# A transformer block in fp32 on one core: constant matmuls at the start, modulation vectors summed on GpSimd, maxima in sixes, five score banks at the end

## The chip, the core and the metric

The kernel runs on one core of a Trainium2 chip. Its engines are TensorE (PE in the profile, its weight loads PEld), VectorE (DVE), ScalarE (ACT), GpSimd (POOL) and SyncE (SP, which here only issues DMAs). The metric is the device time in microseconds, the median of several runs; lower is better.

## The reference

One token batch x of 2048 rows and 512 columns goes through an attention and a gated MLP. Both are modulated by six vectors that come from a condition c:

```
mod = (silu(c) @ w_mod).reshape(1, 6, 1, 512)      # sa, ca, ga, sb, cb, gb
h = layernorm(x) * (1 + ca) + sa
q, k, v = split(h @ wqkv)                          # 32 heads of 16
x = x + ga * (softmax(q k^T / 4) v) @ wo
h = layernorm(x) * (1 + cb) + sb
x = x + gb * ((silu(h @ w_gate) * (h @ w_up)) @ w_down)   # inner width 1792
```

Everything is fp32. The softmax subtracts the maximum of each row of scores.

## The kernel before

**Precision.** A matmul of two fp32 operands is done as three matmuls of rounded parts (high x high, high x low, low x high), collected in one bank of PSUM by `mm3`. With four slices of 128 of the inner dimension this makes 12 matmuls of 128x512 for one bank: a job. The eight banks are tiles `banks[0..7]` (63 to 70 in the lists of instructions below). `Turn` objects hand them out in a fixed circle: `four` for turned tiles and maxima, `bank` for projections and scores, `single` for bank 7.

**Front.** The rows of x come in four chunks of 512. For chunk 0 the row statistics and the normalized rows are made while the first columns of w_mod are loaded in two halves (`wm_ab`). `mod_part` multiplies silu(c) with such a half on TensorE (four 32-row strips side by side, one for each slice of the inner dimension) and copies the result to SBUF as `ev`; `mod_col` turns it into columns and adds the four strips. `turn` transposes the normalized rows; `modulate` scales and shifts them into `h32`, and `half_prep` splits them into the high and low halves `hT`. Jobs of K and Q start as soon as the first half of `hT` is there.

**Projections.** For chunks 0 to 2, `Stream.jobs` writes out the jobs one matmul at a time, and after each matmul `tick` lets other generators ("lanes", each with a period in matmuls) write one step: the splitting of weights (`w`), the preparation of the next chunk (`p`), and the later modulation vectors (`m`, `mods`): vectors 4 and 3 beside chunk 1, vectors 2 and 5 beside chunk 2. What a lane has not done when the jobs are out is written by `finish` behind them. A post of each job copies the bank by ScalarE, subtracts by VectorE (L369) and stores the parts to DRAM (`qd`, `kd`, L372 and L373), all on SP's queue. V stays in SBUF (L395).

**The first maxima.** Scores are computed twice: once (`max_one`, L479) for the maximum of each row (L481, VectorE), and once, transposed, with the maximum as an extra row of the inner dimension, for the exponential (`score`, L526, and ScalarE's L528). The maxima run 21 steps (`LEAD`) ahead of the scores. So 80 maxima stand alone before the first score; they are written between the jobs `late` that remain of the projections (216 matmuls). They need `qop` and `kop`, loaded from `qd` and `kd` on SP's queue (L404). `side` holds small steps that turn a unit's maxima into a row: `max_rows` by TensorE, `max_turned` by VectorE and eight small DMAs.

**Attention and MLP.** `plain` writes steps of score, max and probabilities times V (L541); `filled` writes scores with matmuls of the output projection and MLP of the previous chunk between them (L739). For the last 80 scores there is no max beside them. There `ALONE` gives other places for the MLP's matmuls, and `bank` gets a longer circle. TensorE executes its instructions in the order in which they are written, as does each engine; a `manual_schedule` keeps that order, and semaphores make an instruction wait for what it reads or for the bank that it overwrites.

## Time and profile before

| | us |
|---|---|
| median of three runs (1864.34 to 1866.59) | 1865.5 |
| the profiled execution | 1862.89 |
| its span, first to last instruction | 1861.0 |
| TensorE busy | 1832.9 |
| VectorE busy | 1542.6 |
| ScalarE busy | 1245.7 |
| GpSimd busy | 414.9 |
| first modulation matmul (L279) starts | 10.78 |
| third projection job starts (L209) | 26.65 |
| first max (L479) starts | 127.78 |
| first score (L526) starts | 188.03 |

A busy time is the union of an engine's instructions in the span. A row of the timeline gives the start, the length, the engine, the line, the operation with what it writes and reads, how often in a row it comes, and in brackets how long the engine idled before and what ended that. The chain of waits goes back from the last instruction to what released it; its rows give start, length and what. A row of windows gives, for a stretch of time, the busy time and the number of instructions of PE, PEld, DVE, ACT and POOL, the granted clock of TensorE, the busy share of the DMA engines and the GB/s that they moved. A row of the groups gives the line, engine, operation and shapes, the count, the busy time in us and the mean of one in ns. TensorE's ends are modelled, so its busy time holds short waits too.

### The profile page before, as it was taken

The page shows a single profiled execution, that of the slowest core. Times are in us where ns is not written, and L with a number is a line of the kernel's source. Part 1 is how long each engine was busy: PE and PEld are TensorE (multiplying, and loading weights), DVE is VectorE, ACT ScalarE, POOL GpSimd, SP SyncE. Part 2 cuts the span into 40 slices and gives each one's busy share as a digit, 9 for nine tenths or more (in the row PEclk, how much of TensorE's full clock was granted, in tenths as well). Part 3 has the DMA queues.
Part 4 walks back from the last instruction along what each step waited for, and adds up shares of the span by engine and source line. Part 5 has one row for each costly group of instructions (what it writes and reads, how often), then busy time and mean ns, then how long its engine had stood idle before and what let it go on. Part 6 is the DMA issues. An engine that isn't in the chain of part 4 may idle for free.

```text
span 1861.0 us, 41049 instructions
## 1 busy us (share of the span) xinstructions
PE 1832.9 (98%) x16906; PEld 1152.3 (62%) x16906; DVE 1542.6 (83%) x2588; ACT 1245.7 (67%) x2391; POOL 414.9 (22%) x498
## 2 busy tenths in 40 slices
PE   7999999999999999999999999999999999999999
PEld 5766444444455667666555667666554576666887
DVE  5558999999999889889999998989999998821543
ACT  4231888888887777767877777777878877773211
POOL 3000454446422211111133111111123011130200
PEclk9999999999999999999999999999999999999999
DMA  8855677766853534654454454454633536243642
GB/s 290 292 200 143 175 179 179 202 168 182 218 98 78 142 99 111 166 118 96 105 130 114 106 132 134 123 123 81 165 79 56 113 89 168 76 166 114 260 177 106
DMA packets 80475, 267.62 MB, mean 144 GB/s; under 512 B 19464, under 2 KB 24104, under 8 KB 59608
## 3 DMA queue, kind: packets, MB, share of 16 engines
q1 hardware_dynamic: 61440, 180.10, 33.3%
q0 software_dynamic: 18160, 84.10, 19.1%
q8 instruction: 133, 2.18, 0.5%
q10 hardware_dynamic: 688, 0.80, 0.1%
q14 instruction: 54, 0.44, 0.1%
HBM read 201.85 MB, written 62.13 MB: 142 GB/s over the span
## 4 chain that ended last, share of the span: by engine, by line
PE 93%; DVE 2%; ACT 2%; DMA 2%; SPq 0%; issue 0%; ACTq 0%; DVEq 0%
PE bank L541 27%; PE bank L526 23%; PE bank L739 19%; PE bank L479 10%; PE bank L749 6%; PE bank L209 6%; DVE mx L481 1%; DVE stt L765 1%; PE bank L162 0%; PE bank L723 0%; DMA wm_ab<-in_w_mod 0%; PE bank L491 0%; PE bank L279 0%; DMA kop<-o_dr 0%; DMA rb<-d_dr 0%
## 5 line engine op out<-in xcount | busy, mean ns | idle before, releaser
L481 DVE TENSOR_REDUCE mx<-bank 128x1 f32<-128x512 f32 x2048 | 1283.8, 681 | 104.1 <-PE bank L479 64.8
L479 PE MATMUL bank<-kop,qop 48*128 48x512 f32 x2048 | 745.0, 431 | 3.2 <-DVE mx L481 1.9
L526 PE MATMUL bank<-qop,kop 50*128 50x512 f32 x2048 | 738.1, 427 | 4.6 <-ACT pt__20559 L528 0.5
L526 PEld LDWEIGHTS bank<-qop,kop 50*128 50x128 f32 x2048 | 345.6, 184 | 305.5 <-issue 63.1
L479 PEld LDWEIGHTS bank<-kop,qop 48*128 48x128 f32 x2048 | 343.0, 184 | 29.2 <-DVE mx L481 14.5
L739 PE MATMUL bank<-act,wgu 64*128 64x512 f32 x1872 | 296.8, 392 | 0.0
L739 PEld LDWEIGHTS bank<-act,wgu 64*128 64x128 f32 x1872 | 187.0, 187 | 30.6 <-issue 0.2
L568 POOL TENSOR_TENSOR on<-o,rb 128x512 f32<-128x512 f32 x31 | 39.7, 1282 | 438.2 <-DMA rb<-d_dr 372.5
L739 PE MATMUL bank<-wd,mid 64*128 64x512 f32 x912 | 136.9, 397 | 0.0
L801 POOL CAST mid<-m 128x512 fp32r<-128x512 f32 x40 | 24.3, 609 | 421.9 <-DVE m L799 161.5
L739 PEld LDWEIGHTS bank<-wd,mid 64*128 64x128 f32 x912 | 93.9, 185 | 11.7 <-issue 0.7
L209 PE MATMUL bank<-hT,wqs 128*128 128x512 f32 x384 | 95.6, 399 | 2.3 <-ACT hT L328 1.0
L209 PEld LDWEIGHTS bank<-hT,wqs 128*128 128x128 f32 x384 | 70.3, 188 | 24.3 <-issue 6.1
L797 DVE SCALAR_TENSOR_TENSOR q<-th,bank 128x512 f32<-128x512 f32 x56 | 37.7, 673 | 55.0 <-ACT th L793 55.0
L793 ACT ACTIVATE th<-bank 128x512 f32<-128x512 f32 x56 | 33.2, 594 | 58.4 <-PE bank L749 58.4
L813 DVE TENSOR_TENSOR x<-bank,x 128x512 f32<-128x512 f32 x84 | 53.8, 684 | 20.3 <-PE bank L526 20.2
L369 DVE TENSOR_TENSOR prt<-bank,prt 128x512 fp32r<-128x512 f32 x32 | 22.0, 688 | 46.8 <-ACT prt L367 44.5
L367 ACT CAST prt<-bank 128x512 fp32r<-128x512 f32 x32 | 18.8, 587 | 59.9 <-PE bank L209 46.8
L799 DVE TENSOR_TENSOR m<-bank,q 128x512 f32<-128x512 f32 x56 | 38.7, 691 | 21.1 <-PE bank L749 19.1
L749 PE MATMUL bank<-wd,mid 128*128 128x512 f32 x216 | 52.3, 394 | 0.5 <-DVE mid L802 0.3
L802 POOL TENSOR_TENSOR mid<-m,mid 128x512 fp32r<-128x512 f32 x40 | 51.6, 1289 | 3.3
L739 PE MATMUL bank<-wgu,act 64*128 64x512 f32 x288 | 47.7, 394 | 0.1
(6286 smaller groups left out, 5129.2 us busy)
## 6 DMA issues: line engine op xcount, KB each, us to landing
wgu<-gu_dr SPq DMA_DIRECT2D x48, 1024.0 KB
wd<-wd_dr SPq DMA_DIRECT2D x28, 1024.0 KB
kop<-kd SPq DMA_DIRECT2D x33, 768.0 KB
kop<-kd POOLq DMA_DIRECT2D x29, 768.0 KB, 8.6
gu_dr<-wgu POOLq DMA_DIRECT2D x14, 1024.0 KB, 14.2
kd<-prt SPq DMA_DIRECT2D x16, 512.0 KB
qd<-prt SPq DMA_DIRECT2D x16, 512.0 KB
kop<-gu_dr SPq DMA_DIRECT2D x8, 1024.0 KB
```

The source lines that it names most:

```text
L209: nc.tensor.matmul(pt, lhs(a, k), rhs(b, k), start=(n == 0), stop=(n == 3 * nk - 1))
L479: nc.tensor.matmul(pm, qop[u][rows, s, qt * P:(qt + 1) * P], kop[u % 3][rows, s, kc * CW:(kc + 1) * CW], start=True, stop=True)
L481: nc.vector.tensor_reduce(mx[u][:, b, s, qt, kc:kc + 1], pm, op=ALU.max, axis=AX.X)
L526: nc.tensor.matmul(sp, kop[u % 3][rows, h // 2, kt * P:(kt + 1) * P], qop[u][rows, h // 2, :], start=True, stop=True)
L541: nc.tensor.matmul(pv[u][32 * h:32 * h + 32, cols], v_flat[:, e0:e0 + 32], p_[h][:, cols], start=(kt == 0 and half == 0), stop=(kt == 15), ...
L568: mul.tensor_mul(on, o, rb)
L739: nc.tensor.matmul(outs[e], lhs(e, a, k)[rows], rhs(b, k)[rows], start=(ph == 0 and j == 0), stop=(j == z and (ph == 1 or trade is not None)),
L749: nc.tensor.matmul(outs[e], lhs(e, a, k), rhs(b, k), start=(j == 0), stop=(j == z))
L797: nc.vector.scalar_tensor_tensor(q, th, 1.0, outs[0], op0=ALU.add, op1=ALU.mult)
L799: nc.vector.tensor_mul(m32, outs[1], q)
L802: (nc.gpsimd if slow else nc.vector).tensor_sub(mid[:, 1, :], m32, mid[:, 0, :].bitcast(F32))
L813: nc.vector.tensor_add(ch.x2[:, t, :], outs[e], ch.x2[:, t, :])
```

## The change

Four edits, at the two ends of the program.

1. Front. TensorE gets 14 matmuls of a constant tile (128x256) at the very start, into banks 0 to 3. All four turned tiles of chunk 0 are written ahead of the second `mod_part`. The circle `bank` has four banks for chunk 0. In the first K and Q jobs `mm3` takes two slices of the inner dimension together, with the low half of `hT` last.
2. Vectors 4, 3, 2 and 5 of the modulation are summed on GpSimd (`mod_sum`: four multiplications by silu(c), two additions in place), and TensorE only adds over the 128 partitions: `sum_col` with four matmuls of one column, `sum_row` with one matmul that spreads the sum to all rows. All four run in one lane with a period of 7.
3. The first 80 maxima. Of the late projections 22 instead of 48 matmuls stand ahead of them; then six maxima on six banks and 14 matmuls by turns, the last 12 matmuls behind the maxima. A unit's maxima are taken so that its first 32 use only the first half of the keys. Unit 0's row of maxima is turned by `max_turned`, two side steps at a time.
4. For the last scores the circle of banks is 4, 5, 0, 1, 2 instead of 4, 5, 0, 1, 5, 0, 4, 1.

```diff
+    busy = pa.tile([P, CW], F32, name="busy", tag="h32", bufs=2)
+    nc.vector.memset(busy[:, 0:2 * P], 1.0)
+    for i in range(14):
+        nc.tensor.matmul(banks[i % 4][:, 0:2 * P], busy[:, 0:P], busy[:, 0:2 * P], start=True, stop=True)
...
-    def mm3(pt, lhs, rhs, nk):
+    def mm3(pt, lhs, rhs, nk, by=1):
         n = 0
-        for k in range(nk):
-            for a, b in ((0, 0), (0, 1), (1, 0)):
+        terms = ((0, 0), (0, 1), (1, 0)) if by == 1 else ((0, 0), (1, 0), (0, 1))
+        for k0 in range(0, nk, by):
+            for (a, b), k in product(terms, range(k0, k0 + by)):
...
+    def mod_sum(wm):
+        for k in range(NK):
+            nc.gpsimd.tensor_scalar_mul(wm[:, k, :], wm[:, k, :], sc[:, k:k + 1])
+        nc.gpsimd.tensor_add(wm[:, 0:2, :], wm[:, 0:2, :], wm[:, 2:4, :])
+        nc.gpsimd.tensor_add(wm[:, 0, :], wm[:, 0, :], wm[:, 1, :])
+
+    def sum_col(wm, dst, add):
+        pc_ = single("pcol")
+        for m in range(NK):
+            nc.tensor.matmul(pc_[:, m:m + 1], wm[:, 0, m * P:(m + 1) * P], one, start=True, stop=True)
+        nc.vector.tensor_scalar_add(dst, pc_[:, 0:NK], add)
+
+    def sum_row(wm, dst, factor):
         pr_ = single("prow")
-        nc.tensor.matmul(pr_, quad.to_broadcast([P, P]), ev, start=True, stop=True)
+        nc.tensor.matmul(pr_, one.to_broadcast([P, P]), wm[:, 0, :], start=True, stop=True)
...
+    bank = Turn(4, 5, 6, 7)
+    turn_two(0)
     ev = half_prep(0, ev)
...
+        w4, w3 = load(4), load(3)
+        yield from ticks(9)
+        sum_col(w4, modc[:, 2, :], 1.0)
+        w2 = load(2)
+        yield from ticks(4)
+        sum_col(w3, modc[:, 3, :], 0.0)
+        w5 = load(5)
+        yield from ticks(9)
+        sum_row(w2, ga_bc, 1.0)
+        yield from ticks(3)
+        sum_row(w5, gb_bc, 0.5)
...
         if ci == 1:
-            sm.add("m", 7, mods(4, 3, lambda e, ev: mod_col(ev, [(modc[:, 2 + e], slice(0, NK), 1.0 - e)])))
-        if ci == 2:
-            sm.add("m", 6, mods(2, 5, lambda e, ev: mod_row(ev, (ga_bc, gb_bc)[e], (1.0, 0.5)[e])))
+            bank = Turn(4, 5, 6)
+            sm.add("m", 7, mods())
...
-        s, qt, kc = t // 8, t // 2 % 4, t % 2 * 2 + e
+        s, qt, kc = t // 4 % 2, t % 4, t // 8 * 2 + e
...
     take(late, 22)
     load_k0(last)
-    take(late, 26)
...
-    beside = False
+    beside = True
...
+    four, bank = Turn(0, 1, 2, 3, 6, 7), Turn(4, 5)
     for i in range(-LEAD, -1):
...
-        for r in (0, 2, 1, 3):
+        for k, r in enumerate((0, 2, 1, 3)):
             max_one(4 * (i + LEAD) + r)
-        take(late, 9 if i % 2 else 8)
+            if (4 * (i + LEAD) + k) % 6 == 5:
+                take(late, 14)
         after(i)
-        while side:
+        for f in side[0:2]:
             side.pop(0)()
...
-            places, bank = ALONE.get(places, places), Turn(4, 5, 0, 1, 5, 0, 4, 1)
+            places, bank = ALONE.get(places, places), Turn(4, 5, 0, 1, 2)
```

TensorE's list at the front, up to the first projection matmuls. Before (`wm_ab` is a half of the w_mod columns, `sc` silu(c), `nt` the normalized rows, `ev` the copied result):

```order
L279 MATMUL bank_70<-wm_ab_106,sc 32x512 x4
L162 MATMUL bank_63<-ident,nt 128x128 x4
L162 MATMUL bank_64<-ident,nt 128x128 x4
L288 MATMUL bank_67<-ident,ev 128x128 x4
L279 MATMUL bank_70<-wm_ab_110,sc 32x512 x4
```

The same place after the change, behind the 14 matmuls L272:

```order
L282 MATMUL bank_70<-wm_ab_106,sc 32x512 x4
L162 MATMUL bank_63<-ident,nt 128x128 x4
L162 MATMUL bank_64<-ident,nt 128x128 x4
L291 MATMUL bank_67<-ident,ev 128x128 x4
L162 MATMUL bank_65<-ident,nt 128x128 x4
L162 MATMUL bank_66<-ident,nt 128x128 x4
L282 MATMUL bank_70<-wm_ab_110,sc 32x512 x4
L210 MATMUL bank_68<-hT_147,wqs_114 128x512 x2
L210 MATMUL bank_68<-hT_147,wqs_115 128x512 x2
L210 MATMUL bank_68<-hT_148,wqs_114 128x512 x2
L291 MATMUL bank_70<-ident,ev 128x128 x4
```

The turns into banks 65 and 66 moved ahead of the second half of the modulation; before, they stood behind the first six projection matmuls and the second L288. The low half of hT (148) is now read last.

TensorE's list at the first maxima. Before, with 48 projection matmuls ahead of these rows:

```order
L479 MATMUL bank_63<-kop_87,qop 128x512
L479 MATMUL bank_64<-kop_87,qop 128x512
L479 MATMUL bank_65<-kop_87,qop 128x512
L479 MATMUL bank_66<-kop_87,qop 128x512
L209 MATMUL bank_69<-hT_775,wqs_114 128x512
```

After the change, with 22 ahead:

```order
L510 MATMUL bank_63<-kop_87,qop 128x512
L510 MATMUL bank_64<-kop_87,qop 128x512
L510 MATMUL bank_65<-kop_87,qop 128x512
L510 MATMUL bank_66<-kop_87,qop 128x512
L510 MATMUL bank_69<-kop_87,qop 128x512
L510 MATMUL bank_70<-kop_87,qop 128x512
L210 MATMUL bank_68<-hT_800,wqs_114 128x512
```

Six maxima stand together on six banks, and the projections have only banks 67 and 68 left.

GpSimd's list beside the projections. Before, nothing stands between its last weight split and the attention stage; after the change:

```order
L203 TENSOR_TENSOR wqs_115<-wq_224,wqs_114 128x4x128 x4
L300 TENSOR_SCALAR wm_521<-wm_521,sc 128x512 x4
L301 TENSOR_TENSOR wm_521<-wm_521 128x1024
L302 TENSOR_TENSOR wm_521<-wm_521 128x512
L300 TENSOR_SCALAR wm_529<-wm_529,sc 128x512 x4
```

The same three kinds of rows follow for the other two vectors; TensorE's sums over the partitions (L307, L312) come behind them.

49 lines of the change are left out of this document (23 added, 26 removed).

## Prediction

> **What bounds the kernel now.** I read the page first, then the chain of waits, then the timeline of the three places that the diff touches: the first 30 us, the span from 70 to 190 us, and the span from 1640 to 1695 us.
>
> ```profile
> POOL 3000454446422211111133111111123011130200
> PE bank L541 27%; PE bank L526 23%; PE bank L739 19%; PE bank L479 10%; PE bank L749 6%; PE bank L209 6%; DVE mx L481 1%; DVE stt L765 1%; PE bank L162 0%; PE bank L723 0%; DMA wm_ab<-in_w_mod 0%; PE bank L491 0%; PE bank L279 0%; DMA kop<-o_dr 0%; DMA rb<-d_dr 0%
> 300.00:500.00 200.00, 199.94 (x2008) 93.73 (x2008) 198.62 (x339) 174.44 (x344) 105.23 (x107) 1.00 0.71 186
> ```
>
> GpSimd's busy tenths in 40 slices of 46.5 us stand first, the chain by line second: TensorE carries the span. The third row is a window: 200 us of the attention stage in which TensorE (second number) is busy 199.94 us and VectorE (fourth) 198.62. The change only renames which max comes first there, so I cost that stage at nothing; the same work fills it. What remains are four edits at the two ends of the program, and each is worth what it takes out of TensorE's line there.
>
> **Front: constant matmuls, turns moved, four banks.** The chain of waits (start, length, what):
>
> ```profile
> 10.78 1.94 PE bank L279 x8
> 12.71 1.90 PE bank L162 x8
> 14.61 0.81 PE bank L288 x4
> ...
> 15.99 0.78 ACT h L167
> ...
> 19.59 0.44 PE bank L288 x4
> 20.03 0.89 PE bank L162 x8
> ...
> 70.23 0.99 PE bank L279 x8
> ```
>
> The same eight L279 records cost 1.94 us at 10.78 and 0.99 at 70.23, L162 1.90 then 0.89, L288 0.81 then 0.44: TensorE runs at half speed when it starts, although the granted clock in the window over it reads 1.00 (first row below, last but two). The next L279 is already fast:
>
> ```profile
> 10.00:15.00 5.00, 4.22 (x19) 2.59 (x20) 1.14 (x3) 1.20 (x2) 1.27 (x1) 1.00 0.93 272
> 11.53 0.62 ACT L202 CAST wqs<-wq 128x512 fp32r<-128x512 f32 x1 [2.55 <-DMA wq<-in_A_wqkv]
> 15.34 1.07 PE L279 MATMUL bank<-wm_ab,sc 128*32 128x512 f32 x8
> 26.65 14.15 PE L209 MATMUL bank<-hT,wqs 128*128 128x512 f32 x61 [0.82 <-DVE prt L369]
> ```
>
> So the slow period lasts at most from 10.78 to 15.34, 4.6 us of work. The 14 constant matmuls start when VectorE has written the constant, about 1.2 us by my estimate, since the same memsets run within the first microsecond of the profile. A 128x512 fp32 matmul takes 0.86 us in the chain (L297, below), so 128x256 is 0.43 fast and about 0.8 slow; 4.6 us hold some 5.6 slow ones, the other 8.4 take 3.6 us, end about 9.4. The first w_mod columns are there at 10.78 as before, so nothing is delayed and TensorE idles 1.3 us.
> Then L279 ends at 11.8. ScalarE's copy of its result stands behind the cast of 11.53, which ends at 12.15, so the copy ends at 12.75 and L288 runs 12.76 to 13.2, where it ended at 15.42. The shift into h32 follows 0.57 us later as it does today (15.42 to 15.99): 13.8 for 15.99, **2.2 us**.
> The second pair of turns (0.89 us, 20.03) leaves the place between the second L288 and its scaling and goes where TensorE waits for the first scaling. The by=2 order uses the low half of hT last, so two matmuls less wait for VectorE. The 0.82 us at 26.65, a wait for one of three banks, goes with the fourth bank. Together I take 1.2 of these 1.7 us, since what is late next is VectorE's low halves (two of about 0.69 us in a row). Front: **3.4 us**; bounds 1.2 (the second 1 MB of w_mod is not seen to land before 15.3, and if it lands then only a part of the 2.2 is kept) and 3.9.
> The Trainium skill, "TensorE: Matmul & The Clock Gate" (The HAM clock gate), says that the array starts at half clock, is let up after about 3.4 us of work and falls back after an idle window of the same length. The trace agrees in kind (half speed, at most 4.6 us). By that figure the dummies would end at about 8.9, an estimate from that page.
>
> **Middle: vectors 2 to 5 of the modulation.** Removed from TensorE's line: four L279, two L288, two L297.
>
> ```profile
> 74.65 0.44 PE bank L288 x4
> ...
> 111.80 0.86 PE bank L297 x2
> ...
> 114.04 1.04 PE bank L279 x8
> ...
> 116.36 11.49 PE L209 MATMUL bank<-hT,wqs 128*128 128x512 f32 x48
> ```
>
> Until 114.04 that is 3 x 0.99 + 2 x 0.44 + 0.86 = 4.71 us. The last vector stood at the very end with nothing beside it: from 114.04 to the next L209 at 116.36 are 2.32 us (matmul, copy by ScalarE, matmul). Sum 7.03. Added: two broadcasts of 0.86 = 1.72, and two sum_col of four 128x1 fp32 matmuls. No row shows one of these. With one column to stream, the loads of the stationary set the price: between 0.44 for four (L288) and eight passes at 0.2 us = 1.6; nearest is L162, eight 128-column passes in 0.89, so 0.9 each, 1.8. Net **3.5 us**, bounds 2.1 and 4.4.
> GpSimd covers the sums. Its nearest rows:
>
> ```profile
> L718 POOL TENSOR_SCALAR mid<-x,rs,rs 128x512 f32<-128x512 f32 x12 | 9.1, 783 | 0.3
> L641 POOL TENSOR_TENSOR mid<-mid,gb_bc 128x1024 f32<-128x1024 f32 x7 | 16.8, 2395 | 0.1
> L568 POOL TENSOR_TENSOR on<-o,rb 128x512 f32<-128x512 f32 x31 | 39.7, 1282 | 438.2 <-DMA rb<-d_dr 372.5
> 48.10 1.82 SPq L241 DMA_DIRECT2D wm<-in_w_mod  x2
> ```
>
> 4 x 0.783 + 2.395 + 1.282 = 6.8 us a vector, on an engine that is idle in its second to fourth slice (46 to 186 us). Vectors 4 and 3 are issued about 48 (earlier by the front's gain), and used 63 and 91 L209 later, 15 and 22 us at 0.24, plus the turns between; the sums need two transfers (1 MB each, some 4 us) and 6.8 and 13.6 us. Vectors 2 and 5 have 91 and 84 L209 from load to use, 20 us and more for some 12. What is queued behind each sum on TensorE is the whole projection, so this cover matters (third rival). SP's queue holds the same four loads, two of them earlier.
>
> **The first 80 maxima.** Now 22 instead of 48 L209 stand ahead of the first max, then six maxima and 14 L209 by turns, the last 12 L209 behind them. The side work of unit 0 goes from TensorE (L491 to L493) to VectorE and eight small transfers.
>
> ```profile
> 118.78 0.36 SPq L372 DMA_DIRECT2D qd<-prt  x1
> ...
> 121.23 1.84 SPq L404 DMA_DIRECT2D qop<-qd  x2
> 122.00:123.00 1.00, 1.00 (x6) 0.82 (x5) 0.00 (x0) 0.55 (x1) 0.00 (x0) 1.00 0.03 12
> 123.00:124.00 1.00, 1.00 (x6) 0.84 (x5) 0.69 (x1) 0.04 (x1) 0.00 (x0) 1.00 0.58 197
> 124.00:125.00 1.00, 1.00 (x6) 0.81 (x6) 0.00 (x0) 0.00 (x0) 0.00 (x0) 1.00 0.77 221
> 127.78 0.73 PE L479 MATMUL bank<-kop,qop 48*128 48x512 f32 x4
> ...
> 167.49 2.48 DVE L481 TENSOR_REDUCE mx<-bank 128x1 f32<-128x512 f32 x4 [0.57 <-PE bank L479]
> ...
> 180.11 0.67 PE bank L479 x4
> 180.78 2.02 PE bank L209 x8
> ...
> 188.03 0.49 PE L526 MATMUL bank<-qop,kop 50*128 50x512 f32 x1
> ```
>
> Before: 116.36 to the first score at 188.03, 71.7 us. After, on TensorE: 22 x 0.2394 (11.49 / 48) = 5.3. Then the first max needs qop. Its 393 KB stand in the last column of the windows: little moves from 122 to 123, 197 and 221 KB in the next two, so qop lands near 125.0, 6.2 us after the store at 118.78. That store comes about 1.6 us after the last projection ends (cast 0.59, subtraction 0.69, two hand-overs), so qop lands 7.8 us after it and TensorE stands 7.8 - 5.3 = **2.5 us** in a new wait (bounds 0.6, if qop landed when it was issued, and 4.9, if only at 127.78). Then 80 / 6 = 13.3 groups. VectorE: 6 x 0.62 + 14/12 x 0.69 = 4.5 us while K and Q are projected (7 groups), 3.7 after; TensorE: 6 maxima 1.0 (0.67 for four) and 14 x 0.24 = 3.4, 4.4. Say 4.45: 59.3. Last 12: 2.9. Sum 5.3 + 2.5 + 59.3 + 2.9 = 70.0, **1.7 us** less. Bounds: +5 (a wait of 0.6, groups at 4.3) and -2.7 (4.9 and 4.6). The waits for kop's last piece go, as 32 maxima use only the first two pieces now. Unit 0's eight small transfers are issued some 10 us before the first score, and I take them as hidden.
>
> **End: five banks.** Only the two-job groups with four scores in a row wait. Chain of waits:
>
> ```profile
> 1646.31 0.26 PE bank L526 x2
> 1646.61 0.61 ACT pt__20123 L528
> 1647.26 0.50 PE bank L526
> 1647.76 1.38 PE bank L739 x12
> 1649.38 1.86 PE bank L541 x32
> ...
> 1656.09 1.86 PE bank L541 x32
> ...
> 1661.91 1.86 PE bank L541 x32
> ...
> 1667.76 1.86 PE bank L541 x32
> ```
>
> The fourth score in a row takes the bank whose exp has just begun. Such a group lasts 6.71 us (1649.38 to 1656.09), one with the same twelve steps and no wait 5.85 (1661.91 to 1667.76). There are four. With banks 4, 5, 0, 1, 2 the fourth takes bank 4, free long before. Gain per group between 0.5, TensorE's bare idle time, and 0.86; I take 0.65, since the longer hand-over at the last pair may stay: **2.6 us**, bounds 2.0 and 3.5. ScalarE's eight exps of 0.6 us (4.8) still fit.
>
> **Sum.** 3.4 + 3.5 + 1.7 + 2.6 = 11.2 us. The profiled execution took 1862.89 us (span 1861.0), so 1851.7 after; it stands 2.6 below the median of the runs, and against the median, which is what will be compared, 1865.5 - 11.2 = 1854.
>
> **Rivals.** (A) The maxima lose. If qop lands 4.9 us late and TensorE is slow again behind such a gap (2 us, the front's price), this part costs 2.7 to 4.7 instead of giving 1.7: about 1859. For it: the cover ahead of the first max is cut by 26 L209, 6.2 us. Against: the store ahead of qop leaves earlier than now, since no modulation stands behind it.
> (B) The constant matmuls do not help. All 14 at the slow price take 11 us and end past 12, delaying the weights by 1.4; or they run fast from the start, end near 7.2 and the array slows again before 10.78. The front then gives 0 to 1.2: about 1857. By the page's idle window a gap of 3.4 us would do the second; my gap of 1.3 us is below it.
> (C) Slower: GpSimd's sums come late and TensorE stands in order behind them. Four sums of length S follow one another from about 52; the last is due near 100, so the stall passes the 11.2 us gained once S is about 16 us, 2.4 times the 6.8 of the rows. At 20 us the end would be near 1880. For it: VectorE works beside it half of the time. Against: L568 takes 1.28 us on average in the attention stage, half of a 128x1024 operation, beside a VectorE that is busy 99% of the time. (Most of that reads PSUM, so it says less than it seems.)
> The Trainium skill, "SBUF — State Buffer" (the shared port pair), says that GpSimd and VectorE lock each other out for a whole instruction, which is how S would grow; no row here shows two such operations meet.
> (D) No change: the ends are hidden by work that I do not see. Against it: TensorE has no slack in the window above, and what is taken out ahead of it moves everything.
>
> **Chances.** Forecast (8 to 16 us gained) 0.72, A 0.12, B 0.08, D 0.03, C 0.05. Faster by over 0.2% (3.7 us, about what a measurement of this kernel tells from none): 0.92; within: 0.03; slower: 0.05. All bounds at once give 1848 to 1863; 1848 to 1860 leaves out C, D and the outer edge of A.
>
> **What would show it.** In the profile after: L279's successor at 10.8 us lasting 1.0, first L209 of the third job at 23 rather than 26.65; no TensorE wait on GpSimd at 60 to 110; a wait of TensorE for qop of some 2.5 us ahead of the first max; first score near 179; groups of 5.9 to 6.1 us at the end. I am wrong if the sums are waited for, if qop's wait is over 5 us, or if the end's groups keep 6.7.

## The result: no measurable change, and where the gain went

The changed kernel takes 1864.61 us, the median of 20 executions (1859.32 to 1871.80); the kernel before takes 1865.48 us beside it (20 executions, 1861.57 to 1867.87). The ratio is 0.9996, with a 95% interval of 0.9987 to 1.0004. The prediction was 1854. The profiled execution shown here (1871.80 us, span 1870.0) is the longest of the 20; executions of this kernel differ by how much of their time runs at half clock, which is told below.

The page of the changed kernel, the clock row of its 40 slices and the chain by line; then its row in the view by cores (span, mean granted clock):

```profile
PEclk9989999999999999999999999999999999999999
PE bank L572 26%; PE bank L557 22%; PE bank L770 19%; PE bank L510 10%; PE bank L780 7%; PE bank L210 5%; DMA dn<-o 2%; DVE mx L512 1%; POOL wm L300 1%; DMA wm<-in_w_mod 1%; DVE stt L796 0%; PE bank L813 0%; DMA wd<-wd_dr 0%; PE bank L754 0
```
```profile
core 0: 1870.0 us, clock 0.994
```

TensorE still carries the span, but three names with 1% or more are new on the chain that ended last: the DMA of the denominators (dn), GpSimd's multiplication of the modulation weights (L300) and their load. And the granted clock, 1.000 over the span of the kernel before, is 0.994.

**Front.** TensorE's timeline (start, busy, engine and line, tiles, what ended the idle time before), then VectorE's and GpSimd's at the same place:

```profile
1.18 8.75 PE L272 MATMUL bank<-busy 128*128 128x256 f32 x28 [1.18 <-DVE one L274]
10.20 1.07 PE L282 MATMUL bank<-wm_ab,sc 128*32 128x512 f32 x8 [0.27 <-DMA wm_ab<-in_w_mod]
17.75 1.10 PE L210 MATMUL bank<-hT,wqs 128*128 128x512 f32 x2 [1.45 <-DVE hT L349]
```
```profile
15.93 2.38 DVE L349 TENSOR_TENSOR hT<-h,hT 128x512 fp32r<-128x512 f32 x2
```
```profile
15.88 1.27 POOL L203 TENSOR_TENSOR wqs<-wq,wqs 128x512 fp32r<-128x512 f32 x1 [2.93 <-ACT wqs L202]
```

The constant matmuls end at 9.93 and the first eight L282 take 1.07 us, where they took 1.94. But the two low halves of hT take 2.38 us instead of the 1.29 of the kernel before, beside a GpSimd subtraction that now falls on the same moment, and TensorE waits 1.45 us for them.

**Modulation.** The chain of waits, from the load of vector 2 over its sum and that of vector 5 to the broadcast of vector 5 (L312):

```profile
68.85 11.28 DMA wm<-in_w_mod
...
80.22 6.21 POOL wm L300 x4
...
96.52 2.45 POOL wm L301
...
99.04 1.33 POOL wm L302
...
100.41 1.12 PE bank L312 x2
```

A sum takes 6.21 + 2.4 + 1.3 = 9.9 us instead of the 6.8 predicted, and two follow one another. The load of vector 2 takes 11.28 us from issue to landing, and GpSimd stands idle for the last 5.86 of them. TensorE stands 1.85 us ahead of the broadcast of vector 5. The granted clock in the window from 100 to 105 us is 0.67.

**The first maxima.** TensorE's timeline, and the transfer that it waits for, from the chain:

```profile
122.67 1.65 PE L510 MATMUL bank<-kop,qop 48*128 48x512 f32 x6 [4.07 <-DMA qop<-qd]
124.25 5.70 PE L210 MATMUL bank<-hT,wqs 128*128 128x512 f32 x14
129.88 0.97 PE L510 MATMUL bank<-kop,qop 48*128 48x512 f32 x6
...
134.75 0.73 PE L210 MATMUL bank<-hT,wqs 128*128 128x512 f32 x2 [0.97 <-DVE prt L401]
...
140.27 1.20 PE L210 MATMUL bank<-hT,wqs 128*128 128x512 f32 x4 [1.42 <-DVE prt L401]
...
146.26 1.66 PE L210 MATMUL bank<-hT,wqs 128*128 128x512 f32 x6 [1.86 <-DVE prt L401]
...
191.09 0.49 PE L557 MATMUL bank<-qop,kop 50*128 50x512 f32 x1
```
```profile
118.41 4.21 DMA qop<-qd
```

VectorE's timeline ahead of the second wait for L401:

```profile
135.94 3.68 DVE L512 TENSOR_REDUCE mx<-bank 128x1 f32<-128x512 f32 x6 [1.25 <-PE bank L510]
139.54 0.68 DVE L401 TENSOR_TENSOR prt<-bank,prt 128x512 fp32r<-128x512 f32 x1
```

Three losses stand here one after the other: the wait for qop (4.07 us); behind it six maxima in 1.65 us and 14 L210 in 5.70, which take 0.97 and 3.4 elsewhere; and the waits for the subtraction of a projection (L401), with one more of 0.96 us at 165 us 5.2 us in four. The subtraction stands behind six reductions on VectorE, and TensorE goes on when it ends. The first score of the attention stage starts at 191.09; before, it was 188.03.

**Attention.** VectorE's timeline near 407 us, the transfer ahead of it from the chain, and four windows (length, then busy us with counts of PE, PEld, DVE, ACT, POOL, then granted clock, DMA share, GB/s):

```profile
407.37 0.25 DVE L587 RECIPROCAL dn<-dn 128x16 f32<-128x16 f32 x1 [3.05 <-DMA dn<-o]
```
```profile
391.60 15.75 DMA dn<-o
```
```profile
390.00:405.00 15.00, 15.00 (x156) 6.88 (x155) 14.32 (x24) 13.57 (x28) 11.95 (x15) 1.00 0.94 190
405.00:410.00 5.00, 2.31 (x14) 0.89 (x18) 2.63 (x6) 1.99 (x4) 0.00 (x0) 0.89 0.99 178
410.00:415.00 5.00, 5.00 (x40) 1.94 (x34) 3.04 (x5) 1.57 (x3) 0.00 (x0) 0.50 1.03 378
415.00:420.00 5.00, 5.00 (x50) 2.30 (x50) 4.37 (x8) 4.37 (x9) 0.00 (x0) 0.92 0.39 156
```

VectorE stands 3.05 us with a reciprocal of 128x16 at its head, whose 8 KB took 15.75 us from issue to landing; the reductions behind it are late, TensorE idles 2.7 us, and then it is busy all the time at a clock of 0.50, where steps of four L572 come 0.42 us apart instead of 0.24. The 350th score starts 3.9 us later than in the kernel before, the 400th 9.9 us later. In the kernel before the same reciprocal starts 12.6 us after the issue (387.73 to 400.37) and waits for nothing. This stage was the one that the prediction costed at nothing.

**End.** Chain of waits, one group with four scores in a row:

```profile
1693.97 1.86 PE bank L572 x32
...
1699.90 1.86 PE bank L572 x32
```

From one group to the next are 5.93 us, and no ScalarE stands between; it was 6.71. But at the very end of this profile TensorE waits for the last block of weights, which it does not in the profile of the kernel before, and the clock falls to 0.50 for 3.41 us behind this wait:

```profile
1858.56 7.37 PE L780 MATMUL bank<-wd,mid 128*128 128x512 f32 x24 [1.91 <-DMA wd<-wd_dr]
```

### The profile page after: what moved, and what is told of

It reads as the page before. It is cut to its first block, busy times and chain, and to the rows that moved or that the text cites. A ratio compares the mean times of both kernels' runs of the same rounds, so it can differ in the third digit from the quotient of the medians.

```text
span 1870.0 us, 41067 instructions
## 1 busy us (share of the span) xinstructions
PE 1840.5 (98%) x16904; PEld 1164.2 (62%) x16904; DVE 1553.0 (83%) x2585; ACT 1243.0 (66%) x2386; POOL 455.3 (24%) x522
## 4 chain that ended last, share of the span: by engine, by line
PE 90%; DVE 3%; DMA 3%; ACT 2%; POOL 1%; issue 0%; SPq 0%; ACTq 0%; DVEq 0%
PE bank L572 26%; PE bank L557 22%; PE bank L770 19%; PE bank L510 10%; PE bank L780 7%; PE bank L210 5%; DMA dn<-o 2%; DVE mx L512 1%; POOL wm L300 1%; DMA wm<-in_w_mod 1%; DVE stt L796 0%; PE bank L813 0%; DMA wd<-wd_dr 0%; PE bank L754 0%; DMA wm_ab<-in_w_mod 0%
## 5 line engine op out<-in xcount | busy, mean ns | idle before, releaser
L210 PE MATMUL bank<-hT,wqs 128*128 128x512 f32 x384 | 98.1, 408 | 6.5 <-DVE prt L401 4.2
L210 PEld LDWEIGHTS bank<-hT,wqs 128*128 128x128 f32 x384 | 72.9, 194 | 28.2 <-DVE prt L401 5.5
L780 PEld LDWEIGHTS bank<-wd,mid 128*128 128x128 f32 x216 | 41.3, 193 | 12.7 <-ACT mid L832 2.7
```

Source lines behind the costliest of these rows:

```text
L210: nc.tensor.matmul(pt, lhs(a, k), rhs(b, k), start=(n == 0), stop=(n == 3 * nk - 1))
L780: nc.tensor.matmul(outs[e], lhs(e, a, k), rhs(b, k), start=(j == 0), stop=(j == z))
```

## The experiments

Two theories were set against each other first. **W**: each edit gives or costs what its own place shows, and what was gained is lost in new waits of TensorE and in half clock behind them. **S**: the attention stage, with VectorE at 99% in the window of the prediction, absorbs whatever is gained ahead of it. All runs were repeated beside the kernel before on the same chip. Rows with different times of the kernel before stem from different chips, so two of them are best compared by their differences to it; the changed kernel is 0.9 us below it. "Half clock" is an estimate worked out from the mean granted clock of all executions of a kernel: a stretch at 0.50 loses half of its length, so a mean of c over some 1860 us loses (1 - c) x 1860. Over the 20 executions of the changed kernel the time grows by 0.98 us for each us of this estimate.

| kernel | median us | before, beside it | ratio to before (95%) | mean clock | half clock, us |
|---|---|---|---|---|---|
| changed kernel | 1864.61 | 1865.48 | 0.9996 (0.9987 to 1.0004) | 0.9962 | 7.1 |
| front alone | 1863.09 | 1865.04 | 0.9990 (0.9981 to 0.9999) | 0.9983 | 3.2 |
| modulation alone | 1865.62 | 1865.04 | 1.0003 (0.9991 to 1.0015) | 0.9970 | 5.6 |
| first maxima alone | 1872.72 | 1865.04 | 1.0041 (1.0029 to 1.0054) | 0.9972 | 5.2 |
| end alone | 1862.40 | 1865.04 | 0.9987 (0.9976 to 0.9998) | 0.9984 | 3.0 |
| all but the maxima | 1859.86 | 1865.62 | 0.9964 (0.9950 to 0.9977) | 0.9966 | 6.3 |
| wait for qop filled | 1860.03 | 1865.29 | 0.9974 (0.9965 to 0.9983) | 0.9982 | 3.3 |
| 36 ahead of the maxima | 1864.86 | 1865.29 | 0.9995 (0.9981 to 1.0008) | 0.9934 | 12.3 |
| two-operation multiply | 1863.08 | 1865.29 | 0.9987 (0.9979 to 0.9996) | 0.9966 | 6.3 |
| reciprocal later | 1860.64 | 1865.29 | 0.9979 (0.9970 to 0.9988) | 0.9969 | 5.8 |
| fives on five banks | 1865.13 | 1866.41 | 0.9995 (0.9986 to 1.0005) | 0.9945 | 10.2 |
| split on VectorE | 1864.29 | 1866.41 | 0.9988 (0.9976 to 0.9999) | 0.9965 | 6.5 |
| three mends | 1856.93 | 1866.41 | 0.9954 (0.9942 to 0.9967) | 0.9982 | 3.3 |
| mends, without the maxima | 1853.76 | 1866.41 | 0.9936 (0.9924 to 0.9947) | 0.9984 | 3.0 |
| three mends and fives | 1851.11 | 1865.62 | 0.9920 (0.9907 to 0.9934) | 0.9990 | 1.9 |

The kernel before stands at a mean clock of 0.9986 to 0.9990 in the comparisons with the experiments, 1.9 to 2.6 us.

### Each edit alone

**Front.** The kernel before with the constant matmuls, the turns moved, by=2 and the four banks.

```diff
+    for i in range(14):
+        nc.tensor.matmul(banks[i % 4][:, 0:2 * P], busy[:, 0:P], busy[:, 0:2 * P], start=True, stop=True)
...
+    bank = Turn(4, 5, 6, 7)
+    turn_two(0)
     ev = half_prep(0, ev)
```

> The kernel before with the front edit alone. Theory W (each edit gives what its own place shows, and the gain is lost again in new waits of TensorE at the other places): the profile after puts the turns of chunk 1 at 38.5 us instead of 40.8, so 2.3 us faster than before, 1863.2. Rival S (what is taken out ahead of the attention stage comes back inside it, since VectorE is busy 99% of the time there): no change, 1865.5 within 0.7 us.

Measured: 2.0 us less than before, and the first score at 186.56 against 188.03. The interval reaches from 0.2 to 3.5 us; W's 2.3 lies in it and S's nothing lies just outside. Its profile has a denominators' wait of 0.70 us.

**Modulation.** The kernel before with mod_sum, sum_col and sum_row in the place of the matmuls for vectors 2 to 5.

```diff
-            sm.add("m", 7, mods(4, 3, lambda e, ev: mod_col(ev, [(modc[:, 2 + e], slice(0, NK), 1.0 - e)])))
-        if ci == 2:
-            sm.add("m", 6, mods(2, 5, lambda e, ev: mod_row(ev, (ga_bc, gb_bc)[e], (1.0, 0.5)[e])))
+            sm.add("m", 7, mods())
```

> The kernel before with the GpSimd sums alone. Theory W: the first late projection matmul stood 3.0 us earlier after the full change, 2.3 of it from the front, so 0.7 us is left for this edit, with a wait of TensorE for the last sum (1.9 us) and some 3.5 us of half clock behind it in the profile: 1864.8. Rival S: no change. A third reading, that the wait is of that one execution, gives 3.5 us faster, 1862, with no wait in the profile.

Measured: no change, 0.6 us more. But its first score comes 4.0 us earlier than before, and all but 0.4 us of this is gone by 405 us. Its timelines, TensorE at the first score and VectorE at the denominators:

```profile
184.04 0.50 PE L546 MATMUL bank<-qop,kop 50*128 50x512 f32 x1
```
```profile
398.52 0.25 DVE L576 RECIPROCAL dn<-dn 128x16 f32<-128x16 f32 x1 [1.93 <-DMA dn<-o]
```

From the first score to the end it needs 1676.3 us (span 1860.3), the kernel before 1673.0 (1861.0 - 188.03). TensorE's idle time of 1.6 us at 395 to 400 and half of the 6.8 us at half clock, behind it and at 578, make 5.0, which more than covers these 3.3. At this point S is right about the outcome, and its reason is not the load of VectorE as such: it is one wait at VectorE's head, and the clock.

**The first maxima.** The kernel before with the maxima in sixes, 22 late matmuls ahead of the first, and unit 0's side work on VectorE.

```diff
     take(late, 22)
     load_k0(last)
-    take(late, 26)
...
-        for r in (0, 2, 1, 3):
+        for k, r in enumerate((0, 2, 1, 3)):
             max_one(4 * (i + LEAD) + r)
-        take(late, 9 if i % 2 else 8)
+            if (4 * (i + LEAD) + k) % 6 == 5:
+                take(late, 14)
```

> The kernel before with the new order of the first 80 maxima alone (the circle of banks is turned so that the first two late jobs use banks 5 and 4). Theory W: 4 us of wait for qop, half clock for about 6 us behind it, and waits of the late projections for their two banks: from the first late matmul to the first score 77.8 us instead of 71.7, so 6 us slower, 1871.6. Rival S: the later start is made up in the attention stage, no change. A third reading, that the wait is of that one execution: 1.7 us faster.

Measured: 7.7 us more than before, 1.0041 (1.0029 to 1.0054). W holds. From the first late matmul to the first score are 78.7 us (117.52 to 196.25), 7.1 more than before. Its TensorE timeline has all three losses of the changed kernel at the same sizes, though the three other edits are not in it:

```profile
127.37 1.65 PE L479 MATMUL bank<-kop,qop 48*128 48x512 f32 x6 [4.25 <-DMA qop<-qd]
128.95 5.39 PE L209 MATMUL bank<-hT,wqs 128*128 128x512 f32 x14
...
150.68 1.66 PE L209 MATMUL bank<-hT,wqs 128*128 128x512 f32 x6 [1.87 <-DVE prt L369]
```

**End.** The kernel before with five banks.

```diff
-            places, bank = ALONE.get(places, places), Turn(4, 5, 0, 1, 5, 0, 4, 1)
+            places, bank = ALONE.get(places, places), Turn(4, 5, 0, 1, 2)
```

> The kernel before with the five banks alone. Theory W: the four groups fall from 6.7 to 5.9 us, 3.4 us faster, 1862.1. Rival S says the same here, since nothing lies between this place and the end but the last projection; a rival of its own is that the output's chain of small transfers behind the last scores or the last weight load takes it back: no change, with a wait of TensorE for a transfer behind 1700 us.

Measured: 2.6 us less than before (0.4 to 4.5 by the interval). The groups give 4 x (6.71 - 5.9) = 3.2.

**All but the maxima.** The four single results sum to -2.0 + 0.6 + 7.7 - 2.6 = +3.7 us, and the changed kernel has -0.9. So the edit of the maxima was taken back in the changed kernel, and nothing else touched.

```diff
     load_k0(last)
+    take(late, 26)
...
-        for k, r in enumerate((0, 2, 1, 3)):
+        for r in (0, 2, 1, 3):
             max_one(4 * (i + LEAD) + r)
-            if (4 * (i + LEAD) + k) % 6 == 5:
-                take(late, 14)
+        take(late, 9 if i % 2 else 8)
```

> The changed kernel with one edit taken back, that of the first 80 maxima; the three others as they are, nothing mended. Theory W (the maxima's edit costs what the three others give): the sum of the three alone is -2.0 + 0.6 - 2.6 = -4.0, so 1861.5, with the first score near 182 to 184 and the denominators' wait near 400 in part of the executions. Rival (the three don't add, whatever the maxima do): 1864.6 as the changed kernel.

Measured: 1859.86, 5.8 us less than before (4.3 to 9.3). The three others do add, to a little more than the 4.0 us of their sum, and the maxima's edit costs some 5 us in their company and 7.7 alone. With intervals of 2 to 5 us each, the difference of these two is not resolved. The denominators' wait is there too (2.23 us at 402), and half clock of 6.8 us behind it.

### What the maxima's edit loses

**The wait for qop filled.** The changed kernel with TensorE at work on constants until qop lands, in a bank that the first maximum clears.

```diff
     load_k0(last)
+    for _ in range(16):
+        nc.tensor.matmul(banks[0][:, 0:P], ident, ident, start=True, stop=True)
```

> The changed kernel with 16 constant 128x128 fp32 matmuls (about 3.7 us at full speed) between the 22 late matmuls and the first max, where TensorE waits 4.1 us for qop. They add no time if the wait is what it is. Theory W with the clock: the half speed behind the wait (6.8 us in the windows of the changed kernel, about 3.3 us of time) goes, the wait stays: from the first late matmul to the first score 74.5 us instead of 77.8, 1861.3. Rival: the slow stretch behind the wait is not caused by the gap but by what starts there (six banks at once, transfers): 77.8 stays, 1864.6.

Measured: 1860.03. TensorE's timeline:

```profile
118.48 3.73 PE L894 MATMUL bank<-ident 128*128 128x128 f32 x32
122.35 0.96 PE L510 MATMUL bank<-kop,qop 48*128 48x512 f32 x6
```

The first maximum starts 0.3 us before its time in the changed kernel (122.67); but the six take 0.96 us instead of 1.65, the 14 behind them 3.47 instead of 5.70, and the kernel is 4.6 us shorter. The useless work does not shorten the wait, only keeps the clock up. The waits for L401 stay, 5.2 us, and in this profile half clock of 6.8 us begins behind the third of them instead.

**36 ahead.** The changed kernel with 36 late matmuls instead of 22 ahead of the first maximum. In this order a maximum takes a projection's bank before its result is copied out, so one piece of K and Q is not computed as in the reference.

```diff
-    take(late, 22)
+    take(late, 36)
```

> The changed kernel with 36 instead of 22 late matmuls ahead of the first max; the 12 that stood behind the maxima are used up by this. Theory W: 14 matmuls cover 3.3 us of the 4.1 us wait, the gap is below 1 us and the clock stays: 6.5 us less, 1858. Without the clock's part it would be 3.3 us less, 1861.3. Rival (the two banks of the late projections, not the wait, hold the stage): no change, 1864.6.

Measured: 1864.86, a miss. The wait for qop fell from 4.07 to 0.73 us, and the first score came at 183.17, 7.9 us earlier than in the changed kernel. Then, in windows of the attention stage:

```profile
190.00:195.00 5.00, 5.00 (x32) 2.02 (x28) 3.47 (x6) 3.15 (x6) 0.00 (x0) 0.50 0.99 207
195.00:200.00 5.00, 5.00 (x32) 2.25 (x28) 2.75 (x5) 2.17 (x5) 0.00 (x0) 0.50 1.01 190
...
405.00:410.00 5.00, 4.91 (x29) 2.08 (x33) 3.90 (x7) 1.60 (x4) 0.00 (x0) 0.56 1.03 294
410.00:415.00 5.00, 5.00 (x44) 2.02 (x36) 3.45 (x7) 3.13 (x8) 0.00 (x0) 0.75 0.68 281
```

The granted clock is low from 187 to 201 and from 406 to 412, the second time behind a denominators' wait of 2.65 us, the first time with no gap of TensorE over 0.25 us in the 3 us ahead. Its executions have the lowest mean clock of all kernels here, 0.9934, some 12 us lost.

**Fives on five banks.** The waits for L401 have a cause in the banks: late projections use two by turns, and each waits for the subtraction of the one before the last, which stands behind six reductions on VectorE. Here a third bank goes to them, and the maxima come in fives.

```diff
-    four, bank = Turn(0, 1, 2, 3, 6, 7), Turn(4, 5)
+    four, bank = Turn(0, 1, 2, 3, 7), Turn(6, 4, 5)
...
-            if (4 * (i + LEAD) + k) % 6 == 5:
-                take(late, 14)
+            if (4 * (i + LEAD) + k) % 5 == 4:
+                take(late, 12)
```

> The changed kernel with the first 80 maxima in fives on five banks, three banks for the late projections, 12 late matmuls a group. Theory W (the projection waits for one of two banks, whose subtraction stands behind six reductions): TensorE's waits for the subtraction fall from 5.2 us in 4 to under 1, the wait for qop and the half clock behind it stay, 1864.6 - 4.2 = 1860.4. Rival (VectorE's own load is the bound there: 6 x 0.62 + 0.69 a group, now 5 x 0.62 + 0.69 beside TensorE's 5 x 0.165 + 12 x 0.24 = 3.7): the waits stay at some 4 us in all, and the time at 1864.

Measured: 1865.13, by the time a miss for W. At the place W was right: from the second group on each takes 3.8 us (five maxima and twelve L210 without a gap), no wait for L401 is left, and the first score comes at 186.62 instead of 191.09. TensorE's timeline, VectorE's at the denominators, and two windows:

```profile
127.37 0.96 PE L510 MATMUL bank<-kop,qop 48*128 48x512 f32 x5
128.26 3.01 PE L210 MATMUL bank<-hT,wqs 128*128 128x512 f32 x12
131.21 0.96 PE L510 MATMUL bank<-kop,qop 48*128 48x512 f32 x5
```
```profile
401.57 0.25 DVE L587 RECIPROCAL dn<-dn 128x16 f32<-128x16 f32 x1 [1.90 <-DMA dn<-o]
```
```profile
580.00:585.00 5.00, 4.95 (x36) 2.50 (x39) 4.90 (x13) 2.72 (x7) 2.09 (x11) 0.59 0.01 3
585.00:590.00 5.00, 5.00 (x38) 2.00 (x28) 3.01 (x6) 2.41 (x5) 3.72 (x8) 0.72 0.01 3
```

So 4.5 us were gained at 187 us. Of these 2.0 stand ahead of the first maximum (120.68 against 122.67; this execution has no half clock at 100 us), and 2.5 are the maxima's own: the waits of 5.2 us are gone, but 16 groups of 3.84 us take more than 13.3 of 4.29. All 4.5 were given back: a denominators' wait, and in this execution 14.5 us at half clock after the first score, at 400, at 580 and at the tail. The mean clock of its 11 executions is 0.9945.

### What the other edits lose

**Two-operation multiply.** The changed kernel, GpSimd's multiplication written with a second operation, the addition of zero. The row that priced these (L718, 783 ns) is of that form.

```diff
-            nc.gpsimd.tensor_scalar_mul(wm[:, k, :], wm[:, k, :], sc[:, k:k + 1])
+            nc.gpsimd.tensor_scalar(wm[:, k, :], wm[:, k, :], sc[:, k:k + 1], zero[:, 0:1],
+                                    op0=ALU.mult, op1=ALU.add)
```

> The changed kernel with GpSimd's multiplication written as multiply and add of zero, the form of L718 that took 0.78 us for 128x512 in the kernel before, where the one-operation form took 1.55 us in place. If the form sets the price, a sum takes 6.8 us instead of 10.0, the last sum is there in time, TensorE's 1.9 us wait and 3.3 us of half speed go: 3.5 us less, 1861.1. If the price is that of reading and writing in place, or of VectorE beside it, the row stays at 1.55 us and the time at 1864.6.

Measured: 1863.08. GpSimd's timeline, then TensorE's at the broadcast of vector 5:

```profile
79.73 3.03 POOL L302 TENSOR_SCALAR wm<-wm,sc,zero 128x512 f32<-128x512 f32 x4 [10.57 <-DMA wm<-in_w_mod]
```
```profile
99.47 1.02 PE L315 MATMUL bank<-wm,one 128*128 128x512 f32 x2
99.93 1.02 PE L210 MATMUL bank<-hT,wqs 128*128 128x512 f32 x2
```

With one more operation the instruction takes 0.76 us instead of 1.55. The wait for GpSimd and the half clock behind it are gone; the gain is 1.5 us where W had 3.5, and the interval (0.7 to 3.9 us against the kernel before) does not reach W's number. The half clock that W counted on is not met every time: in the seven profiles with the front edit and the one-operation form TensorE waits 1.40 to 2.43 us for GpSimd, and the clock falls behind two of these waits (1.85 and 2.43).

**The reciprocal three steps later.** The changed kernel, with the reciprocal of the denominators and what follows from it issued three steps later, but for the last unit of a chunk.

```diff
-        i0 = i if u % NG == NG - 1 else i + 2
+        i0 = i if u % NG == NG - 1 else i + 5
```

> The changed kernel with the reciprocal of the denominators (and the two steps behind it) three steps of the attention later for all units but a chunk's last. In the profile of the changed kernel VectorE waited 3.05 us at 404 us for the small transfer that this reciprocal reads, TensorE idled 2.7 us behind it and ran 7 us at half speed. If this wait, met in a part of the runs, is what makes the changed kernel's runs spread from 1859 to 1872 us and its median 4 to 5 us later than its fastest, the median falls by 3 us to 1861.5 and the runs above 1866 go. Rival: the runs spread for other reasons (the wait for qop, the transposing steps): 1864.6 and the same spread.

Measured: 1860.64, 4.0 us less than the changed kernel. VectorE at the denominators:

```profile
407.24 0.25 DVE L587 RECIPROCAL dn<-dn 128x16 f32<-128x16 f32 x1
```

No wait is written behind it, and TensorE neither idles nor slows at 405.

**The split on VectorE.** The changed kernel, the one weight split that met the low halves of hT moved from GpSimd to VectorE, behind them.

```diff
-    split_w(wst0[:, 1], 0)
+    split_w(wst0[:, 1], 0, nc.vector)
```

> The changed kernel with the one split of a weight block that meets the low halves of hT (16 to 18 us) on VectorE, behind them, instead of on GpSimd beside them. Theory W (the two lows take 2.38 us instead of 1.29 because GpSimd's subtraction runs at the same time): the two take 1.3 us, the projections start 1.0 earlier, 1863.6 or so, which the median hardly tells from 1864.6. Rival (another cause, such as the copies of ScalarE beside them): the two stay at 2.4 us.

Measured: 1864.29, which tells nothing by itself. The rows do: VectorE's two low halves, and TensorE's matmuls that wait for them:

```profile
16.83 1.28 DVE L349 TENSOR_TENSOR hT<-h,hT 128x512 fp32r<-128x512 f32 x2
```
```profile
17.56 1.11 PE L210 MATMUL bank<-hT,wqs 128*128 128x512 f32 x2 [0.24 <-DVE hT L349]
```

Without GpSimd beside them the two take 1.28 us, so the 2.38 came from the meeting of the two engines.

### The mends together

**Three mends**: constant matmuls, two-operation multiply, later reciprocal, in the changed kernel.

> The changed kernel with three of the mends at once: 16 constant matmuls (TensorE works through its wait for qop), the GpSimd multiplication in its two-operation form, and the reciprocal of the denominators three steps later. Theory W (each gap of TensorE and the half clock behind it is a cost of its own): the gains add to those of the single mends, -4.6 -1.5 -4.0, so 1864.6 - 10.1 = 1854.5, and no half clock is left but behind the waits for VectorE's subtraction among the first maxima. Rival (the single mends share one gain, because a gap taken away in one place is taken again in a later one): no better than the best single one, 1860.

Measured: 1856.93, between the two theories, and 7.7 us below the changed kernel where the single mends sum to 10.1. By the differences to the kernel before beside each it is 8.6 of 9.5, so the single mends nearly add, as W had it. In its profile the first weights come late, and the constants have run out by then:

```profile
1.18 8.25 PE L272 MATMUL bank<-busy 128*128 128x256 f32 x28 [1.18 <-DVE zero L276]
11.88 1.91 PE L284 MATMUL bank<-wm_ab,sc 128*32 128x512 f32 x8 [2.45 <-DMA wm_ab<-in_w_mod]
```

After 2.45 us without work TensorE takes 1.91 us again for the eight, as in the kernel before. This is the second half of rival B, and it comes in a part of the executions: of the twelve profiles with the front edit two show it, this one and the one with the wait for qop filled (a gap of 2.46 us, then 1.94 for the eight).

**The same without the maxima's edit** (no constant matmuls are needed there).

> The kernel before with the front, the modulation sums (two-operation multiplication) and the five banks at the end, the reciprocal three steps later, and the first 80 maxima left as they were. Theory W: the front alone gave 2.4 and the end 3.1 against the median before, the sums had the first score 4.0 us earlier and lost it again at the denominators, which now come in time: 1865.3 - 9.5 = 1855.8, and no gap of TensorE over 2 us after 30 us. Rival (something in the attention stage gives back what the sums gain, whatever the reciprocal's place): 1865.3 - 2.4 - 3.1 = 1859.8.

Measured: 1853.76, 0.9936 (0.9924 to 0.9947). Between 30 us and the tail TensorE idles under 1 us in every 5 us of its profile; the first score comes at 181.90.

**Three mends and fives.** The kernel of the three mends, with the fives on five banks.

> The changed kernel with fives on five banks for the first 80 maxima, 16 constant matmuls ahead of them, the two-operation multiplication and the reciprocal three steps later. Theory W (the 4.4 us that the fives gained at the first score in the run before were lost in the denominators' wait, 1.6, and in half clock of 14 us behind it): with the reciprocal later and the first wait filled they stay, 1856.9 - 4 = 1853, no half clock among the first maxima. Rival (earlier maxima are given back in the attention stage by another way): 1857, as with sixes.

Measured: 1851.11, 0.9920 (0.9907 to 0.9934), the fastest of all kernels here. Its first maximum and first score, and the window from 100 to 1845 us:

```profile
119.06 0.96 PE L513 MATMUL bank<-kop,qop 48*128 48x512 f32 x5 [0.17 <-DMA qop<-qd]
...
181.24 0.49 PE L560 MATMUL bank<-qop,kop 50*128 50x512 f32 x1
```
```profile
100.00:1845.00 1745.00, 1739.37 (x16494) 1084.42 (x16492) 1490.06 (x2481) 1207.48 (x2324) 396.51 (x476) 1.00 0.52 137
```

The five banks, worth nothing on their own, are worth 5.8 us by the medians, 5.0 by the differences to the kernel before, once the denominators come in time and the other gaps are closed. In the two profiles 3.3 of these lie between the first maximum and the first score (62.2 us against 65.5). So S falls: the attention stage takes a gain made ahead of it, if no wait stands in VectorE's queue. The first score is 6.8 us earlier than in the kernel before, the 1500th 6.9.

## Why the prediction was wrong

**The step that failed is "The first 80 maxima".** The prediction took a gain of 1.7 us; alone the edit costs 7.7, and taken out of the changed kernel some 5. Three terms of its sum:
- The new wait for qop, 2.5 us, measured 4.07 to 4.25. It was inside the bounds (0.6 to 4.9), but the estimate of the landing from GB/s in windows was early: from the first late matmul (113.45) to the first maximum are 9.2 us, not 7.8.
- That TensorE would slow behind the wait stood only in rival A. It did: 1.65 + 5.70 instead of 0.96 + 3.47, 2.9 us. With constants in the wait the slow stretch is gone and the kernel 4.6 us shorter.
- The groups were priced by the load of each engine, 4.45 us. An unhindered group takes 4.29, but with two banks for the late projections a job waits for a subtraction behind six reductions: 5.2 us in four waits, while VectorE itself stands idle 1.25 us and more between its batches. The third bank took all of it away. This wait stood in no rival, so rival A's price for the part, a loss of 2.7 to 4.7 us, was too low as well.

The sum corrected, from the first late matmul to the first score, is 70.0 + 1.6 + 2.9 + 5.2 - 13.3 x 0.16 = 77.6; measured 77.6 (113.45 to 191.09). The prediction's own upper bound for this part comes out of its terms as 5.6 us, not 5 (1.7 + 1.9 + 13.3 x 0.15).

**Front, 3.4 us**: at the turns of the next chunk the changed kernel is 2.3 us ahead (38.48 against 40.80), inside the bounds 1.2 to 3.9; alone it gave 2.0. The clock term was right in kind and size: L282 is fast from the start. What failed is that the waits for the low halves would shrink; they grew to 1.45 us since GpSimd's split now runs beside them. That is what the Trainium skill, "SBUF — State Buffer" (the shared port pair), says of the two engines: the one that is first keeps the pair for its whole instruction, and the other waits. The trace agrees, as GpSimd's subtraction starts 0.05 us ahead of VectorE's, and the run with the split on VectorE agrees: 1.28 us against 2.38. The prediction used the rule for rival C alone and did not ask what the front's new times would put beside each other. Nor is it so that no row of the kernel before shows the two engines meet: there the second of GpSimd's splits starts 0.2 us before the low halves end, and takes 1.35 us where the first takes 1.27.

**Middle, 3.5 us**: the first late matmul came at 113.45 instead of 116.36, 2.9 us for front and middle together, so the middle gave 0.6 in that execution. The price of sum_col was right (0.8 for 0.9). The multiplication was taken from a row of another form, 0.783 us for an instruction of two operations; the one in the change has one and takes 1.55. So a sum takes 9.9 us, and vector 5 came 1.85 us late, with half clock after it: 1.9 + 1.7. The load was mis-sized too: some 12 us were allowed for the load and the sum of a vector, and vector 2 took 11.3 + 10. GpSimd idles 5.86 us for this load, three times what vector 5 was late, so by these rows the sums would have been in time with either term as predicted, which is an estimate; the run with the cheaper multiplication shows it for that term. This is the mechanism of rival C at 9.9 us instead of 16. Where GpSimd was nearly in time (modulation alone, a wait of 0.50) the first score was 4.0 us earlier, as the prediction had it.

**End, 2.6 us**: right and a little small. Groups of 5.9 us give 3.2. The wait for the last block of weights (1.91 us, and 1.7 of half clock behind it) was not reckoned with; waits of 1.6 to 2.3 us for it stand in four of the sixteen profiles, and in none of the end edit alone.

**"The attention stage at nothing"** failed as well. The work is the same, but the reciprocal of the denominators had its 8 KB within 12.6 us in the kernel before, and in the changed one it waits 3.05 us, with 2.7 us of TensorE's time and half clock behind it, 6.0 us in the profile shown. Over all executions it costs about 4 us: the run with a later reciprocal is shorter by that.

**Rival D, no change,** had a chance of 0.03 and is what came, by another way than it named: nothing is hidden; gains of some 6 us in three edits are undone by the fourth and by the clock. By the table the changed kernel lost 7.1 us to half clock and the kernel before some 2. These 5 us are about half of what lies between forecast and result.

**Still open.** At 580 to 590 us (fives) and at 1400 to 1405 (changed kernel) the granted clock falls to 0.59 to 0.72 with no gap of TensorE over 0.25 us in the 3 us ahead of it. The same falls stand at 578 (modulation alone), at 571 (mends, without the maxima), at 1399 (36 ahead) and 4 to 5 us behind the first score (36 ahead, wait for qop filled). In all these places scores and maxima come one at a time, every 0.5 us; no run was made that tells whether this is the cause. Nor is it shown why the fives alone had so much more of it than the fives with mends. It is not shown either why the 8 KB of the denominators take longer in the changed kernel: 13.3 us with the front alone, 14.6 with the modulation alone, at most 12.6 with the maxima alone. And the sum of the four single edits (+3.7) is 4.6 us above the whole (-0.9), of which the intervals hold a part and no run tells the rest.

## What to carry to other kernels

A gap of TensorE of more than 2 us is to be costed at its length and 1.7 or 3.4 us more, for the half clock behind it; one of 1.4 to 2 us cost this in a quarter of the cases here. Several edits that each open a gap of 2 to 4 us can undo gains of the same number, and a useless matmul that fills such a gap is a gain. Where an edit is costed by the load of each engine, the banks between them have to be walked through as well: who writes a bank next, and what stands on the queue of the engine that frees it. A mend that shows nothing on its own may be covered by the next wait in line, so the first score, the wait after it and the clock are to be read apart from the total.

## What the runs showed of the hardware that was not expected

- Half clock sets in behind short gaps: 4.07 us (qop), 2.7 (denominators), 2.45 (late weights), 1.85 (GpSimd's sum), and 1.6 in the run with the modulation alone. It does not do so behind every one. In the sixteen profiles it followed all 13 gaps of 2.15 us and more (the start left out), but only 9 of the 36 between 1.4 and 2 us; the gap of 1.86 us at 144 in the changed kernel left the clock at 1.00.
- But for those that the end of the program cuts off, the low stretches last 3.41 us or a multiple of it (3.41 at 102 us, 6.83 at 122 and at 409 in the changed kernel, 13.65 with 36 ahead). Within one execution they also start at whole multiples of 3.41 us from each other: in the changed kernel at 101.73, 122.21, 408.93, 1402.21 and 1859.60, which are 6, 84, 291 and 134 steps. So how a gap lies to these steps may decide whether the clock falls; no run was made to show it.
- The Trainium skill, "TensorE: Matmul & The Clock Gate" (The HAM clock gate), has the clock fall after an idle window of about 3.4 us; the length of the low stretches agrees, the gap ahead of them does not, as 1.5 to 1.9 us were enough in nine cases.
- On GpSimd a multiplication by a value for each partition takes 1.55 us for 128x512 as one operation and 0.76 us with the addition of zero behind it.
- The 8 KB of the denominators took 15.75 us from issue to landing where the DMA share was 0.94 to 0.99, and at most 12.6 in the kernel before.
